# A fused attention and two-MLP kernel: engine orders written by a planner in the kernel, 40 score steps taken by transposing, another form of a cubic

## The chip, the cores and the metric

The kernel runs on one core of a Trainium2 chip. The metric is device time in microseconds, the median of several executions. TensorE does the matrix products into PSUM, ScalarE (ACT) and VectorE (DVE) the work between them, GpSimd (POOL) starts one group of DMAs and SyncE (SP) the other.

## The reference, cut to what matters

```
scores = (1/S) * z @ z.T                   # 2 batches, S = 3008, z is 3008 x 64
x   = u * (maximum(scores, 0)**2 @ v)      # u, v: 3008 x 256
h   = x @ w_in                             # first MLP (M1): 6016 tokens, 256 -> 2048
P   = a0 + a1*h + a2*h**2 + a3*h**3
Q   = 1 + |b0|*|h| + |b1|*h**2
x2  = (P / (Q + 1e-6)) @ w_out             # 2048 -> 256
h   = x2 @ w2_in                           # second MLP (M2): 256 -> 2048
out = (max(h,0) + alpha*min(h,0)) @ w2_out
```

The weights arrive as float64. The scores of one batch are a symmetric matrix.

## The kernel before

**Precision.** Every matrix operand is held as two float32r parts, `hi` (a rounded copy) and `lo` (what is left), and a product takes three matmuls: hi by hi, lo by hi, hi by lo. `split` makes the two, a cast on ScalarE and a subtraction on VectorE. The scores need two matmuls each: `zA` holds hi of z in its upper 64 rows and lo in its lower, `zB` the two swapped.

**Attention.** Tokens of a batch are taken in six query blocks `(b, j)` of 512 columns (the last has 448), keys in 12 steps `kp` of 256. A score step (`a_scores`) makes two key tiles of 128x512 with four matmuls (L335, L336), then ScalarE takes relu (one instruction for each tile, or one for both) and the square, and hi and lo are split. Three steps later (`LAG_A`) `a_values` adds the step's product with v in 12 matmuls (8 at L377, 4 at L386). The first step is made by `a_first`, a tile at a time. At a block's end the sum is multiplied by u (L422) and stored to DRAM.

**M1 and M2** go through the 6016 tokens in 12 blocks of 512 (the last has 384), each in 8 steps `jp` of 256 hidden units: 12 matmuls make h (`hidden`, L357 to L359), the function is applied, and two steps later 12 matmuls add to the output (`back`). In M1 (`m1_hidden`) three ScalarE instructions read h from PSUM; VectorE builds the cubic as ((a3*h + a2)*h + a1)*h, reading h twice more (L507, L508), and adds a0 inside later instructions (L515, L517); ScalarE makes 1/Q by the square of a reciprocal square root. In M2 (`m2_hidden`) each 128x512 half of h has its own PSUM bank, one ScalarE scale and one VectorE maximum (L561, L562). M1 has one PSUM buffer for h.

**Order.** Python generators interleave the streams: attention alone for 36 steps (`HEAD`), then 40 M1 steps (`X1`) among the remaining 108 attention steps, then M1 and M2 side by side, the last 10 M2 steps alone. The Tile framework orders each engine by priorities (`tc.high_priority`) in this program order. 32 weight tiles are decoded from float64 words by VectorE and ScalarE (`decode`) during the attention; those of M2 go to DRAM and come back when v has been used. Eight warm-up matmuls of 512 columns (L105) run before the first data arrive.

Of the kernel before, what the change touches and what calls it, by code (L numbers as in the profile page):

```python
# [15 lines left out]


BIG, HL, TT, RAW, ZP, XP = 28, 7, 6, 2, 9, 4

WR = 2  # L20
# [3 lines left out]
HEAD, X1 = 36, 40  # L24

RD0, RD = 0.4, 0.55
# [3 lines left out]
SP, AV0, AV1 = 5, 64, 76  # L30

XAHEAD = 2

XLATE = 8

KEEP = 2

EARLY = 100

SOON = 20  # L40

BOUND = 122879.9921875


@with_exitstack
def relu2_attention_rational_mlp_prelu_mlp(
# [12 lines left out]


# [20 lines left out]
    big = ctx.enter_context(tc.tile_pool(name="big", bufs=BIG))  # L81
    xp = ctx.enter_context(tc.tile_pool(name="xp", bufs=XP))
    hlp = ctx.enter_context(tc.tile_pool(name="hlp", bufs=HL))
    tmp = ctx.enter_context(tc.tile_pool(name="tmp", bufs=2))
# [4 lines left out]
    zctx = ExitStack()  # L89
    zp = zctx.enter_context(tc.tile_pool(name="zp", bufs=ZP))  # L90
    wr = zctx.enter_context(tc.tile_pool(name="wr", bufs=WR))
    late = {}

    def raw_tile(nm, early=False):

        if early:
            return big.tile([P, 1024], F32, tag="big", name=nm)
        return tmp.tile([P, 1024], F32, tag="raw", name=nm, bufs=RAW)


    wz = hlp.tile([P, QB], F32R, tag="hl", name="wz")
    nc.vector.memset(wz.bitcast(F32), 0.0)
    wps = psw.tile([P, QB], F32, tag="s", bufs=2, name="wps")
    for i in range(WARM):
        nc.tensor.matmul(wps, wz[:, 0:P], wz, start=i == 0, stop=i == WARM - 1)  # L105


    def split(dst_hi, dst_lo, src, on_act=True):
        if on_act:
            nc.scalar.copy(dst_hi, src)  # L110
        else:
            nc.vector.tensor_copy(dst_hi, src)
        nc.vector.tensor_tensor(dst_lo, src, dst_hi.bitcast(F32), ALU.subtract)  # L113

    def load_rows(t, src, r0, n):

        full, rest = divmod(n, P)
        if full:
            nc.sync.dma_start(
                out=t[:, 0:full, :],  # L120
                in_=src[r0 : r0 + full * P, :].rearrange("(c p) d -> p c d", p=P),
            )
        if rest:
            for p0 in (0, HALF):
                nc.sync.dma_start(
                    out=t[p0 : p0 + rest, full, :], in_=src[r0 + full * P : r0 + n, :]
                )

    vt = {}

    vraw = {}

    def load_v(b, kp):

        if b == 0:
            raw = raw_tile("vraw", True)
        else:
            raw = wr.tile([P, 1024], F32, tag="wr", name="vraw")
        r3 = raw.rearrange("p (c d) -> p c d", c=4)
        r0 = kp * 2 * P  # L140
        load_rows(r3, v[b], r0, min(S - r0, 4 * P))
        vraw[b, kp] = r3

    def split_v(b, kp):
        r3 = vraw.pop((b, kp))
        for i in range(2):
            t = big.tile([P, 2, 2, D], F32R, tag="big", name="vt")
            split(t[:, 0], t[:, 1], r3[:, 2 * i : 2 * i + 2, :], on_act=b > 0 or (kp > 0 and i == 0))
            if kp + i == NKP - 1:

                h2 = t[HALF:P, 0, 1].bitcast(F32)
                nc.vector.tensor_tensor(t[HALF:P, 1, 1], h2, h2, ALU.subtract)
            vt[b, kp + i] = t

    def decode(raw):

        low, high = raw[:, :, 0], raw[:, :, 1]
        w = tmp.tile([P, 2, 512], F32R, tag="t", name="dec", bufs=TT)
        val, ulp = w[:, 0].bitcast(F32), w[:, 1].bitcast(F32)

        nc.vector.tensor_scalar(val, high.bitcast(F32), BOUND, -BOUND, ALU.min, ALU.max)
        nc.scalar.activation(val, val, AF.Copy, scale=2.0**-112)
        vali = val.bitcast(I32)
        nc.vector.tensor_scalar(
            vali, vali, 3, 2**31 - 1, ALU.logical_shift_left, ALU.bitwise_and
        )
        nc.vector.scalar_tensor_tensor(vali, high, -(2**31), vali, ALU.bitwise_and, ALU.bitwise_or)

        nc.vector.tensor_scalar(ulp.bitcast(I32), vali, -(2**23), None, ALU.bitwise_and)
        nc.vector.scalar_tensor_tensor(ulp, low.bitcast(U32), 2.0**-52, ulp, ALU.mult, ALU.mult)  # L170
        nc.vector.tensor_tensor(val, val, ulp, ALU.add)
        return w

    def words(src):
        raw = wr.tile([P, 2, 512], I32, tag="wr", name="wraw")
        if len(w1it) + len(w1ot) < WR:

            nc.gpsimd.tensor_copy(raw[:, 0, 0:1].bitcast(F32), zA[0, 3][:, 0:1].bitcast(F32))
        nc.gpsimd.dma_start(out=raw, in_=src.rearrange("(c p) f -> p c f", p=P))
        return raw.rearrange("p c (n t) -> p (c n) t", t=2)  # L180

    def raw_w(src, jp, wide):

        rows = slice(None) if wide else slice(jp * 256, (jp + 1) * 256)
        cols = slice(jp * 512, (jp + 1) * 512) if wide else slice(None)
        return decode(words(src.bitcast(I32)[rows, cols]))

    def load_w(src, store, jp, wide):
        v3 = raw_w(src, jp, wide)[:, 0].bitcast(F32).rearrange("p (c d) -> p c d", c=2)
        t = big.tile([P, 2, 2, 256], F32R, tag="big", name="w")  # L190
        split(t[:, 0], t[:, 1], v3, on_act=False)
        store[jp] = t

    def spill_w(src, store, jp, wide):

        w = raw_w(src, jp, wide)
        if wide:
            split(w[:, 1], w[:, 0], w[:, 0].bitcast(F32), on_act=False)
        else:
            for c in range(2):  # L200
                f = sg[:, 2 * jp + c : 2 * jp + c + 1]
                lo, hi = w[:, 0, c * 256 : (c + 1) * 256], w[:, 1, c * 256 : (c + 1) * 256]
                nc.scalar.activation(hi, lo.bitcast(F32), AF.Copy, scale=f)
                nc.vector.scalar_tensor_tensor(
                    lo, lo.bitcast(F32), f, hi.bitcast(F32), ALU.mult, ALU.subtract
                )
        d = dr.tile([P, 2, 512], F32R, name=f"wd{wide:d}_{jp}")
        for k in range(2):
            nc.gpsimd.dma_start(out=d[:, k], in_=w[:, 1 - k])
        store[jp] = d  # L210

    def fill_w(store, jp):
        t = late.get("w", big).tile([P, 2, 2, 256], F32R, tag="big", name="w")
        nc.gpsimd.dma_start(out=t.rearrange("p k c d -> p k (c d)"), in_=store[jp])
        store[jp] = t


    sc = const.tile([P, NF + 6], F32, name="sc")
    nc.gpsimd.dma_start(out=sc, in_=cst)
# [516 lines left out]
    for _ in g1s:  # L736
        pass
# [40 lines left out]
```

## Time and profile before

| | us |
|---|---|
| median of 3 runs (lowest, highest) | 1554.02 (1553.92, 1554.23) |
| the profiled execution, first to last instruction (its span) | 1552.0 |
| PE, DVE, ACT, POOL busy within the span | 1545.5, 1397.0, 1189.4, 54.0 |

The profiled execution's own time is given by its span alone; the median of the runs is 2.0 us above it. Busy time of TensorE is not time at its peak: a matmul's record (some 390 ns for 512 columns) overlaps the next one's, so it is the distance between starts that counts.

### The profile page before, as it was taken

Reading aid. Unit: us, or ns where it says so; the run is one execution under the profiler, and the core shown is the slowest. Engines: PE = TensorE matmul, PEld = TensorE weight load, DVE = VectorE, ACT = ScalarE, POOL = GpSimd, SP = SyncE. Lnnn points to the kernel's source line nnn. Section 1 sums busy time; section 2 is a strip of 40 time slices with the busy share of each in tenths; the row PEclk is TensorE's granted clock in tenths of the full one; section 3 lists DMA queues with packets and bytes.
Section 4 is the critical chain, followed back from the end, with each engine's and each line's share of the span. In section 5 each row is a group of like instructions: output and inputs, shape, how many; then the busy total and the mean of one; then the engine's idle time right before and its main releaser. Section 6 shows DMA issues by size and latency. Waiting matters only on the chain.

```text
span 1552.0 us, 18079 instructions
## 1 busy us (share of the span) xinstructions
PE 1545.5 (100%) x6896; PEld 1285.8 (83%) x6896; DVE 1397.0 (90%) x1494; ACT 1189.4 (77%) x1465; POOL 54.0 (3%) x95
## 2 busy tenths in 40 slices
PE   9999999999999999999999999999999999999999
PEld 7888888888888888888788888888888888888888
DVE  8998989999999899898999999998899999898864
ACT  8998988999988889897666766666766666666644
POOL 2010000000000000001000000000000000000000
PEclk9999999999999999999999999999999999999999
DMA  6342111431212212234200000000101010001000
GB/s 204 107 137 75 55 55 42 126 108 34 82 34 68 85 45 68 67 95 124 79 13 30 26 29 22 20 27 28 41 0 42 5 37 28 24 1 42 14 1 24
DMA packets 37767, 83.17 MB, mean 54 GB/s; under 512 B 5152, under 2 KB 14896, under 8 KB 37680
## 3 DMA queue, kind: packets, MB, share of 16 engines
q1 hardware_dynamic: 26128, 48.44, 9.5%
q0 software_dynamic: 11552, 33.57, 7.0%
q8 instruction: 54, 0.88, 0.2%
q14 instruction: 33, 0.27, 0.1%
HBM read 52.70 MB, written 26.48 MB: 51 GB/s over the span
## 4 chain that ended last, share of the span: by engine, by line
PE 94%; DVE 3%; ACT 2%; issue 1%; DVEq 0%; ACTq 0%
PE acc L377 20%; PE acca L377 15%; PE h L358 11%; PE h L357 11%; PE h L359 11%; PE acc L386 10%; PE acca L386 7%; PE s L335 3%; PE s L336 3%; PE acce L367 1%; PE sp L335 0%; PE sp L336 0%; ACT ahi L110 0%; DVE ghi L515 0%; DVE t L507 0%
## 5 line engine op out<-in xcount | busy, mean ns | idle before, releaser
L377 PE MATMUL acc<-ghi,w 128*128 128x512 f32 (+1 forms) x1472 | 365.7, 387 | 0.0
L377 PEld LDWEIGHTS acc<-ghi,w 128*128 128x128 f32 x1472 | 275.3, 188 | 55.0 <-ACT ghi L110 0.6
L358 PE MATMUL h<-xlo,w 128*128 128x512 f32 (+1 forms) x768 | 295.7, 385 | 0.1
L357 PE MATMUL h<-xhi,w 128*128 128x512 f32 (+1 forms) x768 | 295.2, 386 | 0.3 <-DVE m L562 0.2
L359 PE MATMUL h<-xhi,w 128*128 128x512 f32 (+1 forms) x768 | 295.5, 385 | 0.0
L377 PE MATMUL acca<-ahi,vt 128*128 128x512 f32 (+1 forms) x1152 | 288.7, 386 | 0.6 <-DVE ut L422 0.3
L377 PEld LDWEIGHTS acca<-ahi,vt 128*128 128x128 f32 x1152 | 215.9, 188 | 43.5 <-ACT ahi L110 1.2
L501 ACT ACTIVATE sq<-h 128x1024 f32<-128x1024 f32 (+1 forms) x96 | 97.2, 1013 | 151.2 <-PE h L359 147.5
L561 ACT ACTIVATE m<-h,sal 128x512 f32<-128x512 f32 (+1 forms) x192 | 127.2, 680 | 111.4 <-PE h L359 109.9
L386 PE MATMUL acc<-glo,w 128*128 128x512 f32 (+1 forms) x736 | 195.9, 387 | 0.1
L113 DVE TENSOR_TENSOR alo<-r,ahi 128x1024 fp32r<-128x1024 f32 (+2 forms) x133 | 158.1, 1190 | 30.1 <-PE acc L377 14.6
L357 PEld LDWEIGHTS h<-xhi,w 128*128 128x128 f32 x768 | 144.0, 188 | 30.2 <-DVE m L562 1.6
L358 PEld LDWEIGHTS h<-xlo,w 128*128 128x128 f32 x768 | 144.2, 188 | 28.5 <-DVE xlo L113 0.9
L359 PEld LDWEIGHTS h<-xhi,w 128*128 128x128 f32 x768 | 144.1, 188 | 27.4
L113 DVE TENSOR_TENSOR glo<-m,ghi 128x1024 fp32r<-128x1024 f32 (+1 forms) x96 | 115.1, 1199 | 55.6 <-PE acc L377 42.4
L386 PEld LDWEIGHTS acc<-glo,w 128*128 128x128 f32 x736 | 137.8, 188 | 28.2 <-DVE glo L518 0.5
L562 DVE SCALAR_TENSOR_TENSOR m<-h,sg,m 128x512 f32<-128x512 f32 (+1 forms) x192 | 138.0, 734 | 16.7 <-ACT m L561 15.3
L339 ACT ACTIVATE r<-s 128x512 f32<-128x512 f32 (+1 forms) x244 | 138.0, 602 | 19.6 <-DVE t L517 14.5
L342 ACT ACTIVATE r<-r 128x1024 f32<-128x1024 f32 (+1 forms) x143 | 148.9, 1065 | 1.0
L386 PE MATMUL acca<-alo,vt 128*128 128x512 f32 (+1 forms) x552 | 147.6, 385 | 0.0
L110 ACT CAST ahi<-r 128x1024 fp32r<-128x1024 f32 (+2 forms) x133 | 137.3, 1035 | 1.4 <-PE acc L386 0.9
L505 DVE SCALAR_TENSOR_TENSOR ab<-sq,cb,ab 128x1024 f32<-128x1024 f32 (+1 forms) x96 | 120.7, 1257 | 12.8 <-ACT ab L502 12.7
(92 smaller groups left out, 2138.0 us busy)
## 6 DMA issues: line engine op xcount, KB each, us to landing
wraw<-in_moe_w_in_dram POOLq DMA_DIRECT2D x16, 512.0 KB, 4.3
wraw<-in_moe_w_out_dram POOLq DMA_DIRECT2D x16, 512.0 KB, 3.8
wd<-dec POOLq DMA_DIRECT2D x32, 256.0 KB, 2.3
w<-wd POOLq DMA_DIRECT2D x16, 512.0 KB, 3.6
x2d<-x SPq DMA_DIRECT2D x11, 512.0 KB, 2.6
xr<-x2d SPq DMA_DIRECT2D x11, 512.0 KB, 3.2
out_dram<-ot SPq DMA_DIRECT2D x11, 512.0 KB, 2.9
vraw<-in_v_dram SPq DMA_DIRECT2D x10, 512.0 KB, 5.0
```

Source lines behind the costliest of these rows:

```text
L110: nc.scalar.copy(dst_hi, src)
L113: nc.vector.tensor_tensor(dst_lo, src, dst_hi.bitcast(F32), ALU.subtract)
L339: nc.scalar.activation(r[:, i, :n], s, AF.Relu, scale=1.0 / S)
L342: nc.scalar.activation(r[:, :, :n], r[:, :, :n], AF.Square)
L357: nc.tensor.matmul(acc, w_hi, hi, start=first, stop=False)
L358: nc.tensor.matmul(acc, w_hi, lo, start=False, stop=False)
L359: nc.tensor.matmul(acc, w_lo, hi, start=False, stop=last)
L377: nc.tensor.matmul(acc[:, e, :n], w[:, k, i, e * P : (e + 1) * P], hi[i], start=first and i == 0 and k == 0, stop=False,)
L386: nc.tensor.matmul(acc[:, e, :n], w[:, 0, i, e * P : (e + 1) * P], lo[i], start=False, stop=last and i == both - 1,)
L505: nc.vector.scalar_tensor_tensor(ab, sq, b1, ab, ALU.mult, ALU.add)
L561: nc.scalar.activation(t[:, i], h, AF.Copy, scale=sal[:, f : f + 1])
L562: nc.vector.scalar_tensor_tensor(t[:, i], h, sg[:, f : f + 1], t[:, i], ALU.mult, ALU.max)
```

## The change

**Planner.** The kernel now records every operation with an engine, a duration from a formula (for VectorE elements/960 + 0.068 us, and 0.061 more for a column operand; for TensorE columns/2400 + 0.0136 us per matmul), the buffers that it reads and writes, and, for a DMA, a landing time. `Plan.deadlines` gives each a latest start, counted back from TensorE doing its matmuls without a pause in the order in which they were recorded. `Plan.order` runs the list once in time with each engine taking the ready operation with the earliest latest start, gives out 48 SBUF buffers of 4 KB (`PT`) and the others, and the instructions are then emitted in order of their starts, each engine in its planned order (`tc.manual_schedule`). Nothing of the plan acts while the kernel runs: the orders are fixed.

**Mirrored steps.** The scores of key block i against query block j are those of key block j against query block i, transposed. For full blocks with i below j (40 of the 144 steps) the matmuls, relu and square are left out. When the mirror step was made, VectorE turned its 32x32 pieces (`turn_block`), four SP DMAs of 128 KB in runs of 256 bytes stored it to DRAM, and one of 512 KB reads it back; then only the split is done. The query side of the remaining score matmuls reads z through a permuted pattern (`q_side`: 16 runs of 32 columns), and u and the output are permuted outside of the kernel to match.

**M1 and M2.** The cubic is h2*(a3*h + a2) + (a1*h + a0): a fourth ScalarE instruction reads h, VectorE reads none of it, and three VectorE instructions that had a column operand become plain ones. In M2 one VectorE maximum takes both halves of h, from one two-bank buffer; signs of alpha are folded into the weights when they are decoded (16 VectorE products of 128x256). 24 weight casts go from VectorE to ScalarE.

**Other.** `HEAD` is 40 and `X1` 21; M1 steps and weights are added during the attention while recorded VectorE time stays within 4 us of 0.95 of recorded TensorE time. The warm-up is eight matmuls of 128 columns, recorded in the plan. `a_first` goes. The descriptor ring of POOL's DMAs is 2048 bytes.

```diff
-    for i in range(WARM):
-        nc.tensor.matmul(wps, wz[:, 0:P], wz, start=i == 0, stop=i == WARM - 1)
+    def warm(wps):
+        for i in range(WARM):
+            nc.tensor.matmul(wps()[:, 0:P], wz[:, 0:P], wz[:, 0:P], start=i == 0, stop=i == WARM - 1)
...
+    def q_side(z, b, j):
+        if qn[j] < QB:
+            return z[b, j]()[:, : qn[j]]
+        return z[b, j]().rearrange("p (s a r) -> p a s r", s=4, a=4)
...
+    def folded(b, i, j):
+        return i < j and qn[j] == QB
...
+    def turn_block(b, j, kp, r):
...
+        dve(
+            1024,
+            lambda: nc.vector.transpose(
+                t().rearrange("p s a i x -> p i a s x"), r().rearrange("p i (g x) -> p i g x", x=32)
+            ),
...
+        for a in range(4):
+            x0 = a * P + h * 64
+            sp(
+                128,
+                lambda a=a, x0=x0: nc.sync.dma_start(
+                    out=d()[:, :, x0 : x0 + 64].rearrange("s (a r) x -> r (s a) x", r=32),
+                    in_=t()[32 * a : 32 * a + 32].rearrange("r s a i x -> r (s a) (i x)"),
+                ),
...
     def a_scores(b, j, kp):
         n = qn[j]
+        if folded(b, kp // 2, j):
+            r, d = room("rr"), turned[b, kp // 2, j]
+            s0 = kp % 2 * 2
+            sp(512, lambda: nc.sync.dma_start(out=r(), in_=d()[s0 : s0 + 2].rearrange("s p k -> p s k")),
...
+            ahl[b, j, kp] = hi_lo(r, n, kp)
             return
...
+        if folded(b, j, kp // 2):
+            turn_block(b, j, kp, r)
...
-        nc.vector.tensor_tensor(t, t, h, ALU.mult)
-        nc.vector.scalar_tensor_tensor(t, t, a1, h, ALU.add, ALU.mult)
-        nc.vector.scalar_tensor_tensor(hi, t, a0, sq, ALU.add, ALU.mult)
-        nc.vector.scalar_tensor_tensor(t, t, a0, ab, ALU.add, ALU.subtract)
+        act(N, lambda: activation(c(c1), c(h), AF.Identity, scale=a1, bias=a0), [h], [c1], psum=True, ptr=2, **kw)
+        dve(N, lambda: tt(c(t), c(t), c(sq), ALU.mult), [t, sq], [t], **kw)
+        dve(N, lambda: tt(c(t), c(t), c(c1), ALU.add), [t, c1], [t], **kw)
+        dve(N, lambda: tt(c(hi), c(t), c(sq), ALU.mult), [t, sq], [hi], **kw)
+        dve(N, lambda: tt(c(t), c(t), c(ab), ALU.subtract), [t, ab], [t], **kw)
...
-                nc.vector.scalar_tensor_tensor(
-                    t[:, i], h, sg[:, f : f + 1], t[:, i], ALU.mult, ALU.max
-                )
+        dve(2 * n, lambda: nc.vector.tensor_tensor(t()[:, :, :n], h()[:, :, :n], t()[:, :, :n], ALU.max), [h, t], [t])
...
+    with tc.manual_schedule():
+        for o in plan.order():
+            o.fn()
```

## Rows read from the trace of the kernel before

**Rows 1.** The page of the profile: span, busy time (share) and instructions of each engine.

```profile
span 1552.0 us, 18079 instructions
...
PE 1545.5 (100%) x6896; PEld 1285.8 (83%) x6896; DVE 1397.0 (90%) x1494; ACT 1189.4 (77%) x1465; POOL 54.0 (3%) x95
```

**Rows 2.** TensorE weight loads that waited: us in total, times, longest us.

```profile
PEld s L335 <- ACT r L339: 7.8, 31, 0.6
...
PEld acca L377 <- ACT ahi L110: 1.2, 2, 0.7
```

**Rows 3.** Busy time by stretch: length, engines (instructions), granted clock, DMA share, GB/s.

```profile
0.00:12.00 12.00, 10.20 (x33) 7.38 (x34) 7.91 (x17) 7.51 (x12) 2.89 (x11) 1.00 0.85 271
12.00:731.00 719.00, 718.38 (x3182) 592.99 (x3181) 663.92 (x756) 650.35 (x829) 48.51 (x79) 1.00 0.26 81
731.00:1498.00 767.00, 766.71 (x3420) 638.47 (x3419) 701.25 (x691) 507.94 (x591) 2.64 (x5) 1.00 0.08 27
```

**Rows 4.** The chain that ended last: start us, us, what; a steady piece.

```profile
944.93 1.81 PE acc L377 x8
```

**Rows 5.** Instruction groups by form, score matmuls: count, busy us, mean ns, idle before.

```profile
L335 PE MATMUL s<-zA 128*128 128x512 f32 x196 | 78.5, 401 | 0.1
```

**Rows 6.** Instruction groups by form: ScalarE.

```profile
L342 ACT ACTIVATE r<-r 128x1024 f32<-128x1024 f32 x119 | 125.7, 1084 | 0.8
...
L339 ACT ACTIVATE r<-s 128x512 f32<-128x512 f32 x196 | 112.9, 613 | 19.1 <-DVE t L517 14.5 <-PE acca L377 4.6
...
L503 ACT ACTIVATE t<-h,sc 128x1024 f32<-128x1024 f32 x88 | 106.9, 1215 | 0.0
```

**Rows 7.** Instruction groups by form: VectorE.

```profile
L113 DVE TENSOR_TENSOR alo<-r,ahi 128x1024 fp32r<-128x1024 f32 x109 | 132.9, 1220 | 23.3 <-PE acc L377 9.6 <-ACT ahi L110 6.0 <-ACT ab L502 4.2
L562 DVE SCALAR_TENSOR_TENSOR m<-h,sg,m 128x512 f32<-128x512 f32 x176 | 128.1, 745 | 6.9 <-ACT m L561 5.5
...
L517 DVE SCALAR_TENSOR_TENSOR t<-t,sc,ab 128x1024 f32<-128x1024 f32 x88 | 112.7, 1281 | 1.7
...
L508 DVE SCALAR_TENSOR_TENSOR t<-t,sc,h 128x1024 f32<-128x1024 f32 x88 | 112.0, 1273 | 0.6
L518 DVE TENSOR_TENSOR glo<-t,sq 128x1024 fp32r<-128x1024 f32 x88 | 107.5, 1222 | 5.4
...
L204 DVE SCALAR_TENSOR_TENSOR dec<-dec,sg 128x256 fp32r<-128x256 f32 x16 | 7.0, 478 | 0.0
...
L112 DVE CAST w<-dec 128x512 fp32r<-128x512 f32 x16 | 6.8, 425 | 0.2
```

**Rows 8.** Timeline in a busy stretch, two VectorE instructions: start us, us, what.

```profile
300.09 1.27 DVE L508 SCALAR_TENSOR_TENSOR t<-t,sc,h 128x1024 f32<-128x1024 f32 x1
...
301.28 0.68 DVE L113 TENSOR_TENSOR vt<-vraw,vt 128x512 fp32r<-128x512 f32 x1
```

**Rows 9.** Timeline of the head, TensorE.

```profile
1.44 3.78 PE L105 MATMUL wps<-wz 128*128 128x512 f32 x8 [1.44 <-DVE one L224]
...
5.02 1.03 PE L302 MATMUL s<-zA 128*128 128x512 f32 x2
...
6.82 0.39 PE L335 MATMUL sp<-zA 128*128 128x512 f32 x1
...
9.39 1.19 PE L377 MATMUL acca<-ahi,vt 128*128 128x512 f32 x4
```

**Rows 10.** Timeline of the tail.

```profile
1547.70 0.51 PE L367 MATMUL acce<-glo,w 128*128 128x384 f32 x2
```

**Rows 11.** DMA issues by tile: count, KB each, median us from issue to landing.

```profile
xr<-x2d SPq DMA_DIRECT2D x11, 512.0 KB, 3.2
...
zB<-zA SPq DMA_DIRECT2D x18, 128.0 KB, 3.2
...
vraw<-in_v_dram SPq DMA_DIRECT2D x4, 64.0 KB, 4.4
```

More of the change, by code (lines that the diff above doesn't have):

```diff
@@ L129, in relu2_attention_rational_mlp_prelu_mlp @@
[L129 to L153, printed above, removed]
@@ L212, in fill_w, with rooms_of @@
[L212 to L215, printed above, removed]
+    sctx = ExitStack()
+    pss = sctx.enter_context(tc.tile_pool(name="pss", bufs=1, space=PSUM))
+    plan = Plan({"p": PT, "z": ZP, "x": XP, "s": 2, "h": 1, "acc0": 1, "acc1": 1, "m": 1, "sr": 1})
+    def rooms_of(pool, kind, shape, dtype):
+        return [pool.tile(list(shape), dtype, tag=f"{kind}{i}", name=f"{kind}{i}") for i in range(plan.rooms[kind])]
@@ L242, in relu2_attention_rational_mlp_prelu_mlp, with fill_w @@
+    def fill_w(store, jp, in_room):
+        d = store[jp]
+        t = room("w", F32R, (P, 2, 2, 256)) if in_room else big_room("w")
+        pool_dma(
+            512,
+            lambda: nc.gpsimd.dma_start(out=t().rearrange("p k c d -> p k (c d)"), in_=d()),
+            [d],
+            [t],
+            level="load",
+            rate=250.0,
+        )
+        store[jp] = t
     zA = {}
     zB = {}
+    def q_side(z, b, j):
+        if qn[j] < QB:
+            return z[b, j]()[:, : qn[j]]
+        return z[b, j]().rearrange("p (s a r) -> p a s r", s=4, a=4)
@@ L394, in a_values, with lows @@
+        def lows():
+            for i in range(both):
+                for e in range(2):
+                    nc.tensor.matmul(
+                        acc()[:, e, :n],
+                        w()[:, 0, i, e * P : (e + 1) * P],
+                        lo()[:, i, :n],
+                        start=False,
+                        stop=last and i == both - 1,
+                    )
+        pe(n, 8, highs, [w, hi], [acc])
+        pe(n, 2 * both, lows, [w, lo, hi], [acc])
     def a_values(b, j, kp):
@@ L395, in a_values @@
         n = qn[j]
-        if kp == 0:
-            two = j == 1 and not opened
-            acc_a[b, j] = psa.tile([P, ND, QB], F32, tag=f"acc{two:d}", name="acca")
-        acc = acc_a[b, j]
+        first, last = kp == order[b, j][0], kp == order[b, j][-1]
+        if first:
+            acc_a[b, j] = acc_room(int(j == 1 and not opened), "acca")
         hi, lo = ahl.pop((b, j, kp))
-        vk = vt[b, kp]
-        last = kp == NKP - 1
-        pairs(acc, vk, hi, lo, n, kp == 0, last, 1 if last else 2)
@@ L406, in a_u @@
[L406 to L416 removed]
+        pairs(acc_a[b, j], vt[b, kp], hi, lo, n, first, last, 1 if kp == NKP - 1 else 2)
     def a_end(b, j):
@@ L447, in split_x, with three @@
         return hs, ls
+    def three(acc, w_hi, w_lo, hi, lo, first, last):
+        nc.tensor.matmul(acc, w_hi, hi, start=first, stop=False)
+        nc.tensor.matmul(acc, w_hi, lo, start=False, stop=False)
+        nc.tensor.matmul(acc, w_lo, hi, start=False, stop=last)
     def hidden(h, wi, x, n, i):
@@ new lines, in relu2_attention_rational_mlp_prelu_mlp @@
+    n1 = 0
+    for st in range(NB * NKP + 1):
+        edge.clear()
+        next(ga)
+        while extra and plan.debt < DEBT + (EDGE if edge else 0):
+            if st < R0:
+                break
+            what = next((x for x in extra if x[0] == "w" or st >= HEAD), None)
+            if what is None:
+                break
+            if what[0] == "w" and st < HEAD and st - R0 < RD * (sum(x[0] == "w" for x in done)):
+                break
+            extra.remove(what)
+            done.append(what)
+            if what[0] == "w":
+                weight(*what[1], what[2])
+            else:
+                opened.append(n1)
+                next(g1s)
+                next(g1s)
+                n1 += 1
+                edge.clear()
@@ L730, in relu2_attention_rational_mlp_prelu_mlp @@
+    for what in extra:
+        if what[0] == "w":
+            weight(*what[1], what[2])
+    for k, f in enumerate(fills):
+        fill_w(f[1], f[2], False)
     left = (NB - 1) * NJ - KEEP
```

1148 lines of the change are left out of this document (789 added, 359 removed).

## The prediction

> **What bounds the kernel now.** I read the page's engine totals first: TensorE is busy 1545.5 of 1552.0 us, VectorE 1397.0, ScalarE 1189.4 [rows 1]. Since a TensorE record overlaps the next, 100% busy doesn't prove a full engine, so the distance between starts is read next, in the chain that ended last: eight matmuls of 512 columns take 1.81 us in the middle of the kernel, 0.2265 us each [rows 4]. Of the 6896 matmuls 8 are the warm-up; by the code 380 have 448 columns (the two short query blocks) and 384 have 384 (the last MLP block), which leaves 6124 of 512. By columns that is 6124 x 0.2265 + 380 x 0.198 + 384 x 0.170 = 1528 us. The first real matmul starts at 5.02 us [rows 9], the last two start from 1547.70, so 4.1 us of tail follow the last [rows 10]. 1552.0 - 5.0 - 4.1 - 1528 leaves 15 us for everything else: slow clock in the head, waits, handoffs. The list of waits agrees: the largest entry of TensorE's weight loads is 7.8 us in 31 times, for ScalarE's relu to empty a score bank [rows 2]. The reader is to see that TensorE's own work sets the time in every stretch, while VectorE stands at 663.92 of 719 us in the attention stage and 701.25 of 767 in the stage of M1 beside M2 [rows 3]: 92% and 91%, a second limit close behind.
>
> **TensorE's work.** 40 steps lose four score matmuls each, all of 512 columns in a steady stream: 160 of the 6896. Their records look like the others (mean 401 ns, [rows 5], against 390 for the single one in [rows 9]), so each is worth a pitch: 160 x 0.2265 = **36.2 us** less. No matmul is added. Transposing is VectorE's, not TensorE's. The remaining score matmuls of full blocks (80 steps, 320 matmuls) read the moving side in 16 runs of 32 columns instead of one run of 512. The trace has no such read. Between nothing and twice a pitch (0 and 72 us in all) I take nothing: the stream is one column per step either way, and every fp32r row of 512 columns here goes at the same pitch whatever tile it comes from.
>
> **VectorE's work.** In a busy stretch the next instruction starts before the record before it ends: 300.09 + 1.27 = 301.36 against a start at 301.28 [rows 8]. So an instruction costs its mean less 0.08 us. [Rows 7] give the rest:
> M1, per step: three instructions with a column operand (1.273, 1.281 and one like it, the ghi product) become plain ones of 1.222: 0.17 less, 96 steps, 16 us (the eight short steps counted as full). The product with h stays a plain product.
> M2, per step: two maxima of 128x512 at 0.745 - 0.08 become one of 128x1024, which I price like the plain 128x1024 ones, 1.14: 0.19 less, 18 us for 96.
> Weights: 24 casts (0.425 - 0.08) leave, 8 us; 16 products of 128x256 (0.478 - 0.08) come, 6 us.
> Transposes: 40 of 128x1024. No row shows one. The nearest row is the plain 128x1024 subtraction, 1.22, so 1.14 as cost. The lower bound is half of it, as a cast of 512 goes at 0.425 where a plain 512 goes at 0.68 [rows 7, 8]; the upper bound is two passes over the data, 2.3. I take 1.14: 46 us.
> Sum: -16 - 18 - 8 + 6 + 46 = +10, so about 1407 us of VectorE on some 1517: 93% instead of 90%.
>
> By stage, since 19 M1 steps move out of the attention (40 to 21). One M1 step on VectorE is now about 7 x 1.17 = 8.2 us (four like 1.28, three like 1.22, less 0.08 each). Attention: 663.9 + 7.9 [rows 3] - 19 x 8.2 - 4 - 2 + 46 = 556 us. TensorE there: 719 + 7 of work, less 36, less 19 x 24 x 0.2265 = 103, so 587. VectorE stands at 95%. Second stage: 701 + 156 - 75 x 0.17 - 86 x 0.19 = 828 us against 767 + 103 = 870: 95%. Both stay under TensorE, but closer than 92%. TensorE waited little even where VectorE stood at 92% over 719 us, so I charge nothing for it and leave it to a rival.
>
> **ScalarE's work.** Each mirrored step loses two relus (0.613) and a square (1.084), about 2.1 us with overlap: 84 less. A fourth read of h like L503, 1.215 - 0.08 for 96 steps, adds 109; 24 casts of 512 (priced like the relu) 13 [rows 6]. 1189 + 38 = 1227 of 1517, 81%: no bound. M1's only h buffer is freed by ScalarE alone, without the two VectorE reads behind it; that may remove some of the waits, and I count no gain.
>
> **DMA.** 160 stores of 128 KB and 40 loads of 512 KB come in on SP's queue. A mirrored step is used at the earliest in the next query block: some 12 steps of 2.7 to 3.6 us, over 30 us later. A store and a load of near sizes land in 3.2 us each, rows of 64 KB in small pieces in 4.4 us [rows 11]; with the transpose and the issues the chain is about 15 us. The queue is in order, so a store waiting for its transpose holds back the loads of u, z, v and x behind it. DMA engines are 26% busy in that stage [rows 3], and 42 MB more over 590 us is 71 GB/s beside 81. Hidden; without that cover a late load costs TensorE up to the chain's 15 us once.
>
> **Head.** Before, warm-up matmuls fill 1.44 to 5.22 us, and the first ones of the real work still go at 0.43 us per 512 columns (1.03 us for two records that overlap); from 6.82 the record is 0.39 long [rows 9]. 512 columns in 0.43 us are 1.2 GHz, the lower of the two levels, although the granted clock of this stretch reads 1.00 [rows 3]. The full rate began some 4.2 us after steady work did. The new warm-up has a quarter of the columns and ends near 2.3 us, so TensorE stands idle until z is split at 5 us, and I take the same 4.2 us again from there: 2.1 us of work lost, less the 0.6 us that the head lost already. Part of it is covered, because the first values waited for ScalarE (0.7 of the 1.2 us entry, [rows 2], ending at 9.39 [rows 9]); but the first step is no longer made a tile at a time, so its cast comes about 0.5 us later. Sum **+1.5 us**, between 0 and 2.5. The Trainium skill, "TensorE: Matmul & The Clock Gate", Part 1, says that the throttled state is the default and that activity releases it, and advises to warm up first; the 0.43 us rows agree, and by it too the shorter warm-up is a loss.
>
> **Tail.** The last 10 M2 steps run alone before and after, with the same last copies: 4.1 us stay.
>
> **Sum.** 1552.0 - 36.2 + 1.5 = 1517.3 for the span. The median of the runs is 2.0 us above the profiled span, so 1519 us: 2.2% less. What could move it is the 15 us rest: all of the 7.8 us score waits gone gives 1511; as much again in new waits gives 1527.
>
> **Rivals.**
> 1. *VectorE becomes the bound of a stage.* For it: 95% in both stages with a fixed order, and the transpose's price is unknown. In the attention stage the limit is 31 us away, so a transpose of 1.14 + 31/40 = 1.9 us closes it. At the upper bound of 2.3 the stage needs 602 instead of 587: 15 us, 1534. The same size comes if each of the 75 M1 steps of the second stage waits 0.2 us for buffers or VectorE. Against it: the stage before had 92% and next to no waits on VectorE. The Trainium skill, "VectorE: DVE Perf Modes", The three transpose paths, gives 311 ns for 128x128 in bf16; eight of them in one instruction would be an estimated 2.5 us, less 0.08, which makes VectorE's 607 us the bound and the time about 1539. No row here shows the operation, and the plain rows say half of it.
> 2. *The mirrored data come late.* If each of the 40 steps waits 0.9 us for its load, all 36 us are given back: 1554, no change. For it: one queue in order, about 310 DMAs instead of about 110 in some 590 us. Against: 15 us of chain in 30 us of room.
> 3. *Slower: the permuted read costs TensorE.* 320 matmuls; from 36.2/320 = 0.11 us each (half as long again) the gain is gone, at a full extra pitch the time is 1519 + 72 = 1591. Against it: the pitch follows columns alone in every row.
>
> **How the numbers follow.** The forecast gets 0.70 (its own range 1510 to 1528), VectorE or buffers as bound 0.18 (1528 to 1548), the late data 0.04, the slow read 0.05, all else 0.03. Range 1510 to 1542 holds the first and most of the second. About 3 us (0.2%) is what can be told from no change: faster 0.90, same 0.04, slower 0.06.
>
> **What would show it.** Right: 6736 matmuls, the same 1.81 us for eight, score matmuls of the same length as the others, a transpose near 1.2 us, VectorE near 1405 us, a few us of waits in TensorE's list. Wrong: gaps before score matmuls or before the products of mirrored steps, with VectorE or a DMA as releaser; a transpose over 2 us; score matmuls longer than 0.4 us in the new pattern; a first product with v later than 11 us.

## The result and the profile after

The changed kernel takes 1532.7 us (median; 1532.5 to 1535.1), the one before 1554.0 beside it: a ratio of 0.9866 [0.9852, 0.988], 21 us or 1.3% less. The forecast was 1519, so of the 35 us that were expected 21 came. The time lies outside the forecast's own 1510 to 1528 and inside the wider 1510 to 1542. The page of the profile after:

```profile
span 1530.3 us, 17886 instructions
...
PE 1512.1 (99%) x6736; PEld 1261.2 (82%) x6736; DVE 1393.6 (91%) x1429; ACT 1224.8 (80%) x1465; POOL 73.2 (5%) x98
```

Against [rows 1] the 160 matmuls are gone, ScalarE has its forecast 1227 within 3 us, and VectorE is 13 us under its forecast. The transposes cost what the sum took (VectorE groups by form; count, busy us, mean ns, idle before):

```profile
L760 DVE STREAM_TRANSPOSE rt<-r 128x1024 f32<-128x1024 f32 x40 | 49.0, 1236 | 4.1 <-DMA rt<-rt 4.1
...
L1003 DVE TENSOR_TENSOR t<-t,c 128x1024 f32<-128x1024 f32 x88 | 107.8, 1224 | 1.2
```

So the work is as forecast and the time is not. The busy time by stretch (columns as in [rows 3]) says where to look:

```profile
0.00:15.00 15.00, 11.26 (x36) 8.57 (x37) 10.76 (x20) 10.24 (x13) 3.16 (x11) 1.00 0.89 288
15.00:130.00 115.00, 115.00 (x501) 93.78 (x500) 105.68 (x142) 100.77 (x128) 9.18 (x13) 1.00 0.77 204
...
296.00:330.00 34.00, 29.74 (x124) 22.53 (x123) 33.65 (x45) 33.56 (x49) 3.22 (x4) 1.00 0.28 92
...
350.00:366.00 16.00, 14.20 (x55) 11.16 (x54) 9.06 (x13) 11.82 (x17) 1.89 (x3) 0.89 0.85 243
...
660.00:1476.00 816.00, 816.00 (x3643) 681.03 (x3642) 776.43 (x699) 640.75 (x721) 0.00 (x0) 1.00 0.07 24
```

The reader is to see two things. From 660 us on TensorE is full although VectorE stands at 776.43 of 816 (95%). And the losses of the attention stage lie in a few short stretches: around 296 to 330, where VectorE and ScalarE are both full and TensorE is not, and around 356, where TensorE stopped and then went at a lower granted clock. Two full engines do not by themselves make TensorE wait: in the kernel before, a stretch from 300 to 326 us has both as full, and TensorE full as well (same columns):

```profile
300.00:326.00 26.00, 26.00 (x124) 22.95 (x123) 25.67 (x28) 25.60 (x36) 0.00 (x0) 1.00 0.42 120
```

The list of TensorE's waits after names the places:

```profile
PE acc L870 <- DVE ut L914: 4.9, 4, 1.8
PE s L829 <- ACT r L836: 2.2, 4, 0.8
PE acc L881 <- DVE glo L1012: 1.9, 2, 1.7
PE acc L881 <- DVE alo L443: 1.5, 3, 0.7
```

The first line is the new one (its like in the list of before, L377 for L422, is 0.3 us): at a block's end the next block's first product waits until VectorE has multiplied the one attention sum by u (L914). Here is the longest of them in the timeline (columns as in [rows 9]):

```profile
352.23 1.05 ACT L438 CAST ahi<-rr 128x1024 fp32r<-128x1024 f32 x1 [2.07 <-DMA rr<-rt]
353.31 1.23 DVE L443 TENSOR_TENSOR alo<-rr,ahi 128x1024 fp32r<-128x1024 f32 x1 [1.50 <-ACT ahi L438]
...
355.72 0.40 PE L830 MATMUL s<-zB,zA 128*128 128x512 f32 x1
355.97 0.76 DVE L581 TENSOR_TENSOR dec<-dec,sr 128x256 f32<-128x256 f32 x2
356.64 1.22 DVE L914 TENSOR_TENSOR ut<-acc,ut 128x1024 f32<-128x1024 f32 x1
...
357.92 2.10 PE L870 MATMUL acc<-ahi,vt 128*128 128x512 f32 x5 [1.80 <-DVE ut L914]
```

The old block's products start their last matmul before 355.0; four score matmuls (the last is shown) cover 0.9 us, VectorE is still in a weight's sign products (L581), and only then comes u. Where the steps next in line are mirrored, no further score matmul is there to fill the gap.

The delay starts further back, at the first two lines. ScalarE stood idle for 2.07 us until a mirrored tile (`rr`) had come back from DRAM, and VectorE then stood idle for 1.50 us until ScalarE's cast of that tile was done, with the weight's products and u behind it in its fixed order. The sum that u needs was complete soon after 355.0 us, so by this trace most of the stop comes from the late tile; no run takes it out by itself.

**A ledger.** For every matmul I took the distance to the next start, less the steady distance (columns at 2.4 GHz plus 13.2 ns, which is the 0.2265 us of [rows 4] for 512). Excesses over 30 ns are summed as waits (a slow clock counts here too), the smaller ones as pitch. Each row is one profiled execution. The last attention matmul separates the stages.

| us | head, to 15 us | attention | behind it | pitch | span |
|---|---|---|---|---|---|
| before | 3.1 | 5.1 | 1.4 | 5.4 | 1552.0 |
| after | 6.8 | 13.4 | 2.5 | 8.2 | 1530.3 |

The matmuls that left are worth -36.2, the shorter warm-up ones -1.3, waits +13.1, pitch +2.8: together -21.6, and the spans differ by 21.7. Before, waits and pitch make 15.0 us, the 15 us that the prediction had left over. After, of the attention's 13.4 us 6.2 lie between 296 and 330 us, 3.7 are the stop at 356 us with the slow matmuls behind it, and 3.5 are elsewhere. The table closes; what is left to find is why the waits grew, and whether the -36.2 is what the change was about.

### The profile page after: what moved, and what is told of

It reads as the page before. It is cut to its first block, busy times and chain, and to the rows that moved or that the text cites. A ratio compares the mean times of both kernels' runs of the same rounds, so it can differ in the third digit from the quotient of the medians.

```text
span 1530.3 us, 17886 instructions
## 1 busy us (share of the span) xinstructions
PE 1512.1 (99%) x6736; PEld 1261.2 (82%) x6736; DVE 1393.6 (91%) x1429; ACT 1224.8 (80%) x1465; POOL 73.2 (5%) x98
## 4 chain that ended last, share of the span: by engine, by line
PE 87%; DVE 7%; ACT 3%; issue 1%; DMA 1%; SPq 1%; DVEq 0%; ACTq 0%
PE acc L870 33%; PE acc L881 17%; PE h L943 5%; PE h L941 5%; PE h L942 5%; PE m L943 5%; PE m L941 5%; PE m L942 5%; PE s L830 1%; PE s L829 1%; DVE alo L443 1%; PE acc L860 1%; ACT r L836 1%; ACT r L849 1%; DVE vt L443 0%
## 5 line engine op out<-in xcount | busy, mean ns | idle before, releaser
L870 PE MATMUL acc<-ahi,vt 128*128 128x512 f32 (+1 forms) x1152 | 284.8, 389 | 5.8 <-DVE ut L914 4.9
L870 PEld LDWEIGHTS acc<-ahi,vt 128*128 128x128 f32 x1152 | 216.6, 188 | 51.4 <-DVE ut L914 4.8
L997 ACT ACTIVATE t<-h,sc 128x1024 f32<-128x1024 f32 (+1 forms) x96 | 114.1, 1188 | 107.5 <-PE h L943 103.9
L1064 ACT ACTIVATE m<-m,sc 128x512 f32<-128x512 f32 (+1 forms) x182 | 117.8, 692 | 67.9 <-PE m L943 67.7
L943 PE MATMUL h<-xhi,w 128*128 128x512 f32 (+1 forms) x404 | 154.6, 383 | 0.0
L942 PE MATMUL h<-xlo,w 128*128 128x512 f32 (+1 forms) x404 | 154.6, 383 | 0.0
L941 PE MATMUL h<-xhi,w 128*128 128x512 f32 (+1 forms) x404 | 154.6, 383 | 0.0
L881 PE MATMUL acc<-alo,vt 128*128 128x512 f32 (+1 forms) x552 | 147.4, 387 | 1.5 <-DVE alo L443 1.5
L943 PE MATMUL m<-xhi,w 128*128 128x512 f32 (+1 forms) x364 | 140.8, 387 | 0.0
L942 PE MATMUL m<-xlo,w 128*128 128x512 f32 (+1 forms) x364 | 140.8, 387 | 0.0
L941 PE MATMUL m<-xhi,w 128*128 128x512 f32 (+1 forms) x364 | 140.7, 387 | 0.0
L1005 ACT ACTIVATE sq<-ab,one 128x1024 f32<-128x1024 f32 (+1 forms) x96 | 110.3, 1149 | 17.1 <-DVE t L1002 16.8
L1009 DVE TENSOR_TENSOR ghi<-t,sq 128x1024 fp32r<-128x1024 f32 (+1 forms) x96 | 115.5, 1203 | 7.8 <-ACT sq L1006 6.8
```

Of the source, the lines that this page charges most:

```text
L870: nc.tensor.matmul(acc()[:, e, :n], w()[:, k, i, e * P : (e + 1) * P], hi()[:, i, :n], start=first and i == 0 and k == 0, stop=False,)
L881: nc.tensor.matmul(acc()[:, e, :n], w()[:, 0, i, e * P : (e + 1) * P], lo()[:, i, :n], start=False, stop=last and i == both - 1,)
L941: nc.tensor.matmul(acc, w_hi, hi, start=first, stop=False)
L942: nc.tensor.matmul(acc, w_hi, lo, start=False, stop=False)
L943: nc.tensor.matmul(acc, w_lo, hi, start=False, stop=last)
L997: act(N, lambda: activation(c(t), c(h), AF.Identity, scale=a3, bias=a2), [h], [t], psum=True, ptr=2, **kw)
```

## The experiments

All times are medians; the kernel before took 1553.9 to 1554.1 beside each. The last column is the ledger of each run's one profiled execution.

| run | us | ratio to before | waits: head, attention, behind |
|---|---|---|---|
| after | 1532.7 | 0.9866 [0.9852, 0.988] | 6.8, 13.4, 2.5 |
| e3_no_mirror | 1579.6 | 1.0166 [1.0149, 1.0183] | 10.9, 17.9, 2.5 |
| e8_old_cubic | 1574.1 | 1.0127 [1.0112, 1.0142] | 7.2, 22.9, 32.4 |
| e10_plan_only | 1620.8 | 1.0428 [1.0412, 1.0443] | 10.5, 27.6, 33.8 |
| e11_turn_twice | 1571.6 | 1.0111 [1.0094, 1.0128] | 7.0, 52.6, 2.5 |
| e6_dve_short | 1526.9 | 0.9827 [0.9814, 0.984] | 6.8, 9.0, 1.1 |
| e5_act_short | 1537.3 | 0.9895 [0.9881, 0.9908] | 6.7, 17.7, 3.0 |
| e5b_act_short | 1529.8 | 0.9844 [0.9829, 0.9859] | 6.8, 11.3, 1.3 |
| e4_u_short | 1528.8 | 0.9837 [0.9822, 0.9851] | 6.6, 9.9, 2.5 |
| e2_plain_read | 1528.8 | 0.9836 [0.9822, 0.9851] | 6.7, 13.7, 2.5 |
| e1_warm512 | 1532.9 | not told from after | 6.0, 13.8, 2.5 |
| e7_ban | 1525.0 | 0.9817 [0.9804, 0.983] | 6.5, 5.7, 2.4 |
| e9_best | 1520.1 | 0.9782 [0.9769, 0.9796] | 5.9, 1.6, 2.0 |

### Undoing the parts: mirroring and the cubic

```diff
     def folded(b, i, j):
-        return i < j and qn[j] == QB
+        return False
```

> All 144 score steps are computed, nothing is transposed; planner, cubic, M2 form, head and permuted read stay as in the changed kernel (1532.7 us). Theory A (mirroring itself gives the full 36 us, and the planned order with its head, its read and its waits costs some 14 us whether or not steps are mirrored): 1532.7 + 36.2 = 1569, within 4 us, so 15 us slower than the kernel before, with waits again near the change of batch. Rival B (the mirrored steps bring the new waits, so mirroring gives only 21 us): about 1554, the time of the kernel before.

Neither theory's number: mirroring is worth 46.8 us, more than its matmuls (by the ledger 36.2 of matmuls, 8.6 of waits and 2.3 of pitch), and without it the rest of the change is 25.5 us slower than the kernel before. So something in "the rest" costs much and something else must pay for it. The next one puts the old cubic into the planned kernel:

```diff
-        act(N, lambda: activation(c(c1), c(h), AF.Identity, scale=a1, bias=a0), [h], [c1], psum=True, ptr=2, **kw)
...
-        dve(N, lambda: tt(c(t), c(t), c(sq), ALU.mult), [t, sq], [t], **kw)
-        dve(N, lambda: tt(c(t), c(t), c(c1), ALU.add), [t, c1], [t], **kw)
+        dve(N, lambda: tt(c(t), c(t), c(h), ALU.mult), [t, h], [t], **kw)
+        dve(N, lambda: stt(c(t), c(t), a1, c(h), ALU.add, ALU.mult), [t, h], [t], ptr=1, **kw)
```

> M1 computes its cubic in the old form inside the planned kernel: three ScalarE reads of h, two VectorE reads, four VectorE instructions with a column operand; orders planned anew. Nothing is left out. VectorE gets some 16 us more, ScalarE 109 us less, h's only PSUM buffer is freed later. By the planner's run the end is the same (1517.25 against 1517.33), the waits at the change of batch 3.6 + 1.5 us and some others. Theory A (the cubic's form is worth little by itself): 1530 to 1536. Theory B (h's single buffer, freed late by two VectorE reads, makes TensorE wait in M1 steps, which the planner's run doesn't show): over 1540. Theory C (ScalarE relieved where attention runs beside M1): under 1528.

Theory B, and far beyond its bound: 41.4 us slower. Its weight loads that waited behind 660 us, and the busy time of that stretch:

```profile
PEld h L941 <- DVE t L1002: 20.9, 22, 2.4
PEld m L941 <- DVE m L1069: 9.9, 11, 2.7
```

```profile
660.00:1476.00 816.00, 797.59 (x3490) 651.75 (x3489) 758.48 (x670) 551.94 (x627) 0.00 (x0) 1.00 0.07 24
```

VectorE is less busy than after (758.48 against 776.43), ScalarE much less, and yet TensorE starts 153 matmuls fewer in the stretch. It is no engine's total load, then; two thirds of the listed waits are for M1's one h buffer. By the ledger 30 of the 41 us are lost behind the attention and 9.5 in it. The timeline at 831 us:

```profile
831.13 1.21 DVE L1001 TENSOR_TENSOR t<-t,h 128x1024 f32<-128x1024 f32 x1
...
832.93 1.07 PE L881 MATMUL acc<-glo,w 128*128 128x512 f32 x4
833.39 1.01 ACT L995 ACTIVATE sq<-h 128x1024 f32<-128x1024 f32 x1
...
834.44 1.28 DVE L1002 SCALAR_TENSOR_TENSOR t<-t,sc,h 128x1024 f32<-128x1024 f32 x1 [1.50 <-ACT sq L995]
...
835.77 0.50 PE L941 MATMUL h<-xhi,w 128*128 128x512 f32 x1 [1.78 <-DVE t L1002]
```

The next h waits for L1002, the last of five reads of the old one. Counted over the M1 steps that begin between 740 and 1400 us, the time from the first start to the last end of the reads of one h is 6.7 us here (median) in steps 11.3 us apart, and 4.2 us in steps 10.9 us apart after. The kernel before needed even 8.1 us, but its steps were 13.4 us apart: it had put 40 M1 steps into the attention and had 56 left for this stage, where the planned kernels have 75. Filling h takes 12 x 0.2265 = 2.7 us more, so one pass through the buffer is 9.4 us with the old cubic and 6.9 with the new one, of the 10.9 us that the 48 matmuls of an M1 and an M2 step take. The wait of before for this read is 0.4 us in its list. The fourth corner takes both out:

> No mirrored steps and the old cubic, so the arithmetic of before except for M2's single maximum and its signs; what stays of the change is the planner with HEAD 40 and at least 21 M1 steps. Nothing is left out. The run without mirroring took 1579.6 and had 18 us of planned waits and 34 in all. Theory A (those 25 us over before come from the planner's orders and placement, not from the cubic): 1573 to 1582. Theory B (they come from ScalarE's fourth read of h, 109 us on an engine that then makes all 144 steps' relus and squares): 1554 to 1565.

Theory A was right in kind and much too small: 1620.8 us. The four corners add up almost exactly (differences of the unrounded medians):

| us | mirrored | not mirrored | mirroring |
|---|---|---|---|
| new cubic | 1532.7 | 1579.6 | -46.8 |
| old cubic | 1574.1 | 1620.8 | -46.7 |
| cubic's form | -41.4 | -41.3 | |

From before (1554.0) the orders, the earlier end of the attention with its 75 M1 steps behind it, the single maximum of M2, the permuted read and the smaller edits together cost +66.8; the new cubic gives 41 back and mirroring 47. In the ledger of e10, beside the one of before, the waits are up by 7.4 us in the head, 22.5 in the attention and 32.4 behind it, and the pitch by 7.1; which of these edits brings which was not tried.

### How much room VectorE and ScalarE have

Every transpose is made twice (the rest unchanged):

```diff
-            lambda: nc.vector.transpose(
+            lambda: [nc.vector.transpose(
                 t().rearrange("p s a i x -> p i a s x"), r().rearrange("p i (g x) -> p i g x", x=32)
-            ),
+            ) for _ in range(2)],
```

> Every transpose is done twice into the same tile, one more 1.24 us VectorE instruction in each of the 40 mirrored pairs, about 1.15 us with overlap, 46 us in all; orders as after, nothing is left out. Tests how far VectorE is from being the bound of the attention stage. Theory A (the sum of the prediction: VectorE has 31 us of room there, then it is the bound): 15 us more, 1548. Theory B (fixed orders and short buffers let little of the room be used, each added instruction comes through): 1565 to 1578. Theory C (the added work fits where transposes lie, because most of them are in the blocks before M1 and weights fill VectorE): 1533 to 1540.

38.8 us more, inside theory B's range. The attention stage's waits go up by 39.2 us, for some 46 us of added work. Some 7 us of that are matmuls at the lower clock behind longer stops: 40 go 0.43 us apart behind the head, against 7 after. The stretch that had no wait after shows it (busy time by stretch):

```profile
15.00:130.00 115.00, 108.63 (x457) 85.91 (x456) 110.69 (x139) 88.76 (x111) 7.94 (x11) 0.99 0.69 180
```

VectorE rises from 105.68 to 110.69 of 115 and TensorE falls from 115.00 to 108.63: the "31 us of room" at 95% were not to be had, with these orders. The other direction takes 64 instead of 512 columns per half in one M1 subtraction:

```diff
-        dve(N, lambda: tt(c(t), c(t), c(ab), ALU.subtract), [t, ab], [t], **kw)
+        dve(N, lambda: tt(t()[:, :, :64], t()[:, :, :64], ab()[:, :, :64], ALU.subtract), [t, ab], [t], **kw)
```

> The last subtraction of P in an M1 step (cubic less its rounded copy times Q) takes 64 of 512 columns in each half, the rest is left out; all orders as after. It takes about 1.0 us of VectorE off each M1 step, 21 in the attention stage and 75 behind it. Theory A (VectorE at 95% in both stages is where TensorE's waits come from): waits for u, the splits and the planned decode at 300 to 330 us fall by 2 to 4 us and glo's 1.9 us goes: 1527 to 1530. Theory B (only the few moments at a block's end matter, in which an attention product itself is late, and the second stage had no waits to lose): 1531.5 to 1533.

5.8 us less, theory A by a hair below its range: 4.4 of waits in the attention stage and 1.4 behind it. Little of it is at the change of batch (6.2 to 5.7 us between 296 and 330); most is at the block ends, where the stop at 356 us shrinks from 2.0 to 0.8 us and no slow matmuls follow. The 75 steps from 660 us on have nothing to gain, TensorE being full there with or without. For ScalarE the first attempt misfired:

```diff
-        act(N, lambda: activation(c(c1), c(h), AF.Identity, scale=a1, bias=a0), [h], [c1], psum=True, ptr=2, **kw)
+        act(N, lambda: activation(c1()[:, :, :64], h()[:, :, :64], AF.Identity, scale=a1, bias=a0), [h], [c1], psum=True, ptr=2, **kw)
...
-        dve(N, lambda: tt(c(t), c(t), c(c1), ALU.add), [t, c1], [t], **kw)
+        dve(N, lambda: tt(c(t), c(t), c(sq), ALU.add), [t, c1], [t], **kw)
```

> The fourth ScalarE read of h takes 64 of 512 columns in each half, and the sum behind it uses the square instead, so a0 + a1*h is left out of the cubic; all orders as after. It takes about 0.95 us of ScalarE off each M1 step, 92 us in all. Theory A (ScalarE's new read is what makes it late where attention runs beside M1, at the change of batch above all): the waits for relu fall, 2.2 to 1 us, and the time by 2 to 5 us, 1528 to 1531. Theory B (ScalarE at 80% is no bound, VectorE alone holds TensorE up): 1532 to 1533.5.

4.6 us slower, with less work. The edit itself had put in a wait, as ScalarE's groups show:

```profile
L1005 ACT ACTIVATE sq<-ab,one 128x1024 f32<-128x1024 f32 x88 | 102.0, 1159 | 38.0 <-DVE t L1003 20.3 <-DVE t L1002 17.6
```

The reciprocal square root (L1005) writes over the square, which the sum (L1003) now read; after, that line idles 15 us and never for L1003. With `tt(c(t), c(t), c(t), ALU.add)` in its place, and the reads that the planner is told of left as they were:

> As in e5_act_short the fourth ScalarE read takes 64 of 512 columns in each half, but the sum behind it now adds t to itself instead of the square, so that the reciprocal square root, which overwrites the square, has nothing new to wait for (in e5 ScalarE's line 1005 idled 20 us behind that sum). Left out: a0 + a1*h in the cubic. Orders as after. Theory A (e5 was slower by its own new wait; relieving ScalarE by itself helps where attention runs beside M1): 1528 to 1531. Theory B (ScalarE is no bound anywhere, only the new wait counted): 1532 to 1533.5. If it stays at 1537, the new wait was not the cause.

2.9 us less, in theory A's range, but not at the change of batch, which the theory of e5 named above all: between 296 and 330 us the waits stay at 6.2 us, and only one of these reads lies there. In the ledger 1.2 us come off behind the attention, and of the 2.1 in it 1.6 are slow matmuls that do not follow a stop of the same length at 358 us. So it is not shown that ScalarE's fourth read makes the waits at the change of batch. That the misfire cost 7.5 us beside it shows that the length of M1's chain counts, not only the two engines' load.

### A block's end, the permuted read and the head

```diff
-            lambda: nc.vector.tensor_tensor(t()[:, :, :n], acc()[:, :, :n], t()[:, :, :n], ALU.mult),
+            lambda: nc.vector.tensor_tensor(t()[:, :, :64], acc()[:, :, :64], t()[:, :, :64], ALU.mult),
```

> At the end of a query block VectorE multiplies only 64 of 512 columns of each half by u (the rest of x is left as u itself); every planned order is unchanged. That instruction then takes about 0.3 us instead of 1.2. Theory A (four block ends make TensorE wait for this product before the next block's first product may write the one accumulator, some 5.6 us with a drop of the clock worth 1.5 us behind the longest): the waits at 136, 301, 356 and 412 us shrink by about 0.9 us each and the drop of the clock goes: 4 to 5 us less, 1528. Rival B (VectorE comes to the product late because other work is queued ahead of it): 1 us less at most.

3.9 us less: the wait for u is real, and shortening VectorE's product shortens it. TensorE's distances ahead of the next block's first product lose 2.8 us in all. The stop at 356 us is still there with 1.1 us, and the matmuls behind it go at the full rate, with a granted clock of 1.00 from 350 to 366 us.

```diff
-        return z[b, j]().rearrange("p (s a r) -> p a s r", s=4, a=4)
+        return z[b, j]()
```

> The query side of the full blocks is read in one run of 512 columns instead of 16 runs of 32; the mirrored tiles then stand in another column order than the computed ones, so this kernel leaves out the permutation. Every planned order is unchanged. Theory A (the permuted pattern costs 6 ns for each of 320 matmuls): score matmuls start 227 ns apart instead of 233, time 1.9 us less, 1530.8. Rival B (the 6 ns come from something else, the mixture of shapes or the score banks): the distance stays 233 and the time stays.

3.9 us less too, twice theory A's 1.9, which counted the score matmuls alone. The waits are much the same; the pitch column falls from 8.2 to 3.4 us. In the chain that ended last one step of after, and the same step with the plain read:

```profile
61.92 0.23 PE s L829
62.15 0.23 PE s L830
62.39 0.23 PE s L829
62.62 0.23 PE s L830
62.85 1.85 PE acc L870 x8
```

```profile
61.04 0.23 PE s L829
61.26 0.23 PE s L830
61.49 0.23 PE s L829
61.72 0.23 PE s L830
61.94 1.81 PE acc L870 x8
```

From the first score matmul to the first product it is 0.93 us against 0.90, and the eight products behind them take 1.85 against 1.81. By these two pieces, rounded as they are, that is 0.07 us per step and 5.6 us for 80 steps. The means over the attention (233 against 227 ns for a score matmul, 1.851 against 1.822 us for the eight) give some 4 us, the pitch column 4.8.

```diff
-            nc.tensor.matmul(wps()[:, 0:P], wz[:, 0:P], wz[:, 0:P], start=i == 0, stop=i == WARM - 1)
+            nc.tensor.matmul(wps(), wz[:, 0:P], wz, start=i == 0, stop=i == WARM - 1)
```

> The eight warm-up matmuls have 512 columns again instead of 128; every planned order is unchanged. Theory A (the head lost 2 us to the lower clock): the score matmuls of the first steps go at 0.23 us instead of 0.43 soon after 5 us, the first product with v starts near 9.7 us instead of 11.4, and the time falls by 1.5 to 2 us to about 1531. Rival B (the head is bound by ScalarE and VectorE after the first data, so a faster TensorE only waits longer): the first product with lo parts starts at 14 us as before and the time stays at 1532.7.

No gain. In its timeline the score matmuls go 0.23 us apart from 7.1 us on, where after has 0.43 until 10.2, and still the first products come late, the ones with hi 0.5 us earlier than after and the ones with lo 0.6 us later (first pair of lines after, second e1):

```profile
11.38 2.00 PE L870 MATMUL acc<-ahi,vt 128*128 128x512 f32 x8
14.13 1.21 PE L881 MATMUL acc<-alo,vt 128*128 128x512 f32 x4 [0.74 <-DVE alo L443]
```

```profile
10.87 2.11 PE L870 MATMUL acc<-ahi,vt 128*128 128x512 f32 x8 [0.83 <-ACT ahi L438]
14.72 0.96 PE L881 MATMUL acc<-alo,vt 128*128 128x512 f32 x3 [1.75 <-DVE alo L443]
```

### Planning the waits away

The planner's own run of the list already has most of these waits (some 6 us between 297 and 320). It counts VectorE's time when it adds M1 steps, not ScalarE's. No M1 step and no weight between attention steps 68 and 74:

```diff
-            if st < R0:
+            if st < R0 or 68 <= st < 74:
```

> No M1 step and no weight is recorded between attention steps 68 and 74, the stretch where one batch hands over to the next; everything else as after, orders planned anew. Theory A: the some 5 us of TensorE waits between 296 and 326 us come from M1 and weight work placed in a stretch where attention with its own transposes already fills VectorE and ScalarE. The planner's own run then holds 3 us less of waits there and ends 4.3 us earlier, so the waits of that stretch fall from 5 to about 2 us and the time from 1532.7 to 1528.5 (1527 to 1530). Theory B: those waits come from the new batch's data (z, v, u by DMA and their splits), which the ban does not touch: 1532 to 1533.5, and the releasers there are then splits of z and v that wait for transfers.

7.7 us less, more than theory A said. Half of it is where theory A looked: between 296 and 330 us the waits were 6.2 us, and 2.3 are left around the change of batch. Another 3 us are at the next block's end, where the stop of 2.0 us shrinks to 0.6 and no slow matmuls follow; the orders were planned anew for the whole kernel. The stretch of the change of batch:

```profile
296.00:330.00 34.00, 32.34 (x141) 26.22 (x141) 33.55 (x41) 32.93 (x49) 2.12 (x2) 1.00 0.47 111
```

And with wider limits, another `HEAD` and `X1`, two of the planner's constants (PACE from 25 to 30, EDGE from 4 to 8) and warm-up matmuls of 512 columns:

```diff
-HEAD, X1 = 40, 21
+HEAD, X1 = 38, 22
...
-            if st < R0:
+            if st < R0 or 66 <= st < 78:
```

> The ban as in the run before, between steps 66 and 78, two attention steps fewer and one M1 step more ahead of the second stage (HEAD 38, X1 22), PACE 30 and EDGE 8 in the planner, and warm-up matmuls of 512 columns. No arithmetic is changed. Theory A (the waits lie already in the plan and can be planned away without touching the arithmetic): the planner's own end is 9.5 us earlier, so 1523 (1520 to 1527), TensorE's waits after the head 8 us where there were 18. Theory B (what is planned doesn't carry to the chip: the fixed orders meet other durations and new waits arise): 1530 to 1534.

1520.1 us: 33.8 less than before and 12.6 less than after, with the same arithmetic. The attention's waits are 1.6 us where before had 5.1. What is left at the top of TensorE's list, apart from the start, is the head and one block's end:

```profile
PE acc L881 <- DVE alo L443: 1.3, 1, 1.3
PE acc L870 <- DVE ut L914: 1.3, 1, 1.3
```

## Why the prediction was right, and what was mis-sized

**TensorE's work** was right: 6736 matmuls, 160 x 0.2265 = 36.2 us, and the ledger closes with it.

**The waits** are the term that was mis-sized. The prediction saw VectorE at 95% in both stages, charged nothing for it, and let the rest of 15 us move by 7.8 either way. The span is 13.0 us above the forecast 1517.3: waits in the attention +8.3 and behind it +1.1, pitch +2.8, and the head 0.9 more than was taken. The 7.8 were waits of weight loads; TensorE's own list of before has no entry for that relu, and the ledger has 5.1 us for the attention's waits of every kind, so 1511 was never within reach by them. That the time lies near the first rival's 1534 is luck. Neither of its conditions came: a transpose takes 1.24 us, and the second stage waits 1.1 us more, not 15. The attention stage has the waits, at places that an average over the stage can't show: the change of batch (e7), the block ends (e4), and slow matmuls behind one of them. The first rival's deciding point, a transpose of 1.9 us, was far too high: e11 loses 39 us at twice 1.24, where the prediction's sum had 15. Room read from a stage's busy share was taken for time that can be used.

**The cubic** was the largest thing overlooked. "I count no gain" is wrong by 41 us in the planned orders (e8); what the new form would bring in the orders of before no run shows. The trace had what was needed: steps 13.4 us apart with five reads of h over 8.1 us, and a change that puts 75 instead of 56 such steps into the second stage. At the new distance the old chain waits and the new one doesn't. The total came out as near as it did because terms that were not in the sum, +67, -41 and the 10 us that mirroring brings beyond its matmuls, cancel down to some 15. That is luck too. That the longer hold of h is the whole of the 32 us behind the attention in e8 isn't shown: the list gives it 20.9 of weight loads' waits, and M2's maximum 9.9. Nor was it tried which part of the +67 comes from the single maximum of M2.

**The permuted read** was put at nothing, with 72 us as the far bound. It costs 3.9 us in time (e2). Part of it is hidden in the ledger's +2.8, since attention before had a pitch excess of its own.

**The head** was put at +1.5 us and came to +2.4 (3.7 of waits less 1.3 of warm-up). The first product with v is at 11.38 us instead of 9.39 [rows 9], past the 11 us that the prediction named as a sign of trouble. But its reason falls: e1 gets the full rate back three microseconds earlier and gains nothing, because ScalarE's cast and VectorE's subtraction set when the products start. What else makes the new head later (the first step taken whole, or the planned orders) was not tried. The Trainium skill, "TensorE: Matmul & The Clock Gate", has the advice to warm up first under "Why this matters for your kernels" and for benchmarks, not in Part 1 as the prediction has it. A full-width warm-up is seen to work in the clock in e1, and there it buys no time.

**Transposes** were right: 1.236 us each, as a plain 128x1024 instruction. The 2.5 us estimated from the Trainium skill, "VectorE: DVE Perf Modes", The three transpose paths, is twice what this trace has.

**Late mirrored data** did not come as a bound, and a slower kernel did not come. No DMA is among the releasers of TensorE's waits. But ahead of the longest of them a mirrored tile was late, 2.07 us for ScalarE and 1.50 for VectorE, and two transposes stood 4.1 us in all until earlier stores had landed (the line L760 above). The prediction's 15 us of chain in over 30 us of room leaves these out, and a list of TensorE's releasers alone hides them, because VectorE's order passes the delay on.

## What to carry to other kernels

A change in several parts is a sum only against a schedule: take each part out on the chip, since one may be there to pay for another (here +67, -41 and -47). Before moving work into a denser stage, compare how long one step holds its only buffer with the distance of steps there; the busy share of the engines doesn't show it. When orders are planned, read the plan's own gaps first: keeping M1 steps and weights out of the change of batch was worth 7.7 us for one line. But the plan does not show everything: its end was the same with either cubic, and the chip's times are 41 us apart. When TensorE waits for an engine, follow that engine's own idle time back as well; the cause may stand two engines away.

## What the runs showed of the hardware

A moving side read in 16 runs of 32 columns (128 bytes) costs a 512-column matmul about 6 ns (233 against 227), and the eight matmuls with plain operands behind such a step some 30 ns together (1.851 against 1.822 us, after and e2); which part inside TensorE makes the latter isn't shown. After the 2.0 us stop at 355.7 us TensorE's matmuls went 0.427 us apart for about three microseconds, the lower of its two levels, though they had gone at full rate for the 30 us ahead of the stop; the granted clock of 350 to 366 us reads 0.89. The stop alone does not decide it: e1 has the same orders and the same stop, and its matmuls go at the full rate at once, at a granted clock of 1.00 (busy time by stretch, and the first products behind the stop):

```profile
350.00:366.00 16.00, 14.21 (x63) 11.31 (x62) 9.31 (x13) 12.36 (x17) 1.89 (x3) 1.00 0.87 250
```

```profile
358.46 2.09 PE L870 MATMUL acc<-ahi,vt 128*128 128x512 f32 x8 [1.79 <-DVE ut L914]
```

So a single profiled execution can differ by some 1.5 us there. In the head the distance of 0.427 us stands beside a granted clock of 1.00, as before, so the distance is the surer sign.
